# Seven block products from the third block on, earlier scores, and own banks for y: a retention layer and its feed-forward on one core

## The chip, the cores and the metric

The kernel runs on one NeuronCore of a Trainium2 chip. The core has five engines with queues of their own: TensorE (PE in the profile) multiplies matrices, its weight loads are listed apart (PEld); VectorE (DVE), ScalarE (ACT) and GpSimd (POOL) work element by element; SyncE (SP) issues transfers, which 16 DMA engines carry out. Each engine takes its own instructions in order and waits on semaphores for the others. The metric is the time of one execution in device microseconds; three runs before the change took 208.76, 208.87 and 209.04 us, median 208.87.

## The reference

Four sequences of 768 steps with eight heads of 64 go through a recurrent state that decays by a factor of its head; the result, with the heads side by side, is the input of a two-layer feed-forward net with g = h·tanh(softplus(h)) (Mish).

```python
gamma = 1.0 - 2.0 ** (-5.0 - np.arange(H))
for t in range(S):
    state = gamma[None, :, None, None] * state + np.einsum('bhd,bhe->bhde', k[:, :, t], v[:, :, t])
    y[:, :, t] = scale * np.einsum('bhd,bhde->bhe', q[:, :, t], state)
...
x = np.ascontiguousarray(attn_out.transpose(0, 2, 1, 3)).reshape(B * S, H * D)
h = x @ w_in
sp = np.where(h > 20.0, h, np.log1p(np.exp(np.minimum(h, 20.0))))
g = h * np.tanh(sp)
return (g @ w_out).astype(np.float32)
```

q, k and v are 4 x 8 x 768 x 64, w_in is 512 x 2048, w_out 2048 x 512, the output 3072 x 512, all float32.

## The kernel before

**Chunks and blocks.** The 3072 steps are 24 chunks of 128, six to a sequence. Chunks are grouped into blocks: block 0 has four (0 to 3), blocks 1 to 10 have two each: block 1 has 4 and 5, block 2 has 6 and 7, block 3 has 8 and 9, and so on to block 10 with 22 and 23. Blocks are numbered from 0 here, so the third block is block 2. The code's `first[blk]` is a block's first chunk, `a` or `g` a chunk.

**What a chunk needs first.** q, k and v are loaded (line 128, on SP's queue, three transfers of 256 KB), cast to 16 bits with their decay factors on GpSimd (`casts`, lines 223 to 231), and q and k are turned (transposed) by a DMA on SP's queue (`turn_by_dma`, line 235). This text calls the turn of chunk n by DMA Tn; there are 18, T6 to T23. `next_chunk(g)` casts up to chunk g, issues Tg and then loads further chunks, so many ahead of g as `load_to` says: chunks below g+3, g+4 or g+5. Stores of finished output tiles (line 179) go through the same SP queue. They are put on a list with a unit number and are issued by `store_due` when the program reaches that unit.

**A block's attention.** `get_ready(blk)` puts on TensorE the outer products k·v (u, line 401) and the scores k·q (at, line 394) of both chunks; the scores read the turned q and k. `settle` then works on DVE: `mid` and `sth` (lines 436, 438, 445, 447: the states in the middle and at the end of a chunk) and `am`, the masked scores (line 459). `leave` makes the state after the block's second chunk (nothing for the last chunk of a sequence). `retain` multiplies the states with q (`past_of`), `finish` the masked scores with v (`present_of`); both add up in y in PSUM, which is then copied to xt, the input of the feed-forward net: one half by DVE (line 526), one by ACT (line 528). `retain` also has a one-element copy to `seen` on DVE (line 514).

**A block's feed-forward.** The first product is cut in units: each unit (`g1`, line 541) is eight matmuls of 128x256 for two rows of h, followed by Mish on ACT (line 549). Blocks 1 to 10 have eight units, numbered 0 to 7. In blocks 1 and 2 the second product is 32 matmuls of 128x512 in eight more units, 8 to 15 (`g2_mm`, line 555; `g2_out`, line 559 copies the result out). From block `SEVEN` = 3 on it is made in the manner of Strassen and Winograd with seven products of half size, 56 matmuls of 128x256 (`seven`, line 615). It needs sums of g made on DVE: S1 and S2 in halves in `sums_a` (lines 604, 605), S3 in `sums_b` (609), S4 in `sums_c` (613), all in the tile gsum; sums T1 to T4 of the second weight (`weight_sums`, eight operations, lines 588 to 591, tile tmat), made once in the block before the first that uses them; and snapshots of partial results on ACT (line 641). Its order on TensorE is A11·B11, A12·B21, S1·T1, S2·T2, then the `retain` of the next block, S3·T3, the `finish` of the next block, S4·B22, A22·T4.

**Who comes when.** `manual_schedule` keeps the order of the program on each engine. `plan_of(blk)` says at which unit of a block the next block's attention, casts, turns and loads are put between the units. In block 1 that is get_ready at unit 10, in block 2 at unit 7, in blocks 3 to 6 at unit 3. From block `ONE` = 6 on the scores of the block after next are put into the seven products, interleaved with the states of the next (`retain` with `later`), and `settle` follows at unit 0 of the next block.

**PSUM.** The pool mm has three banks for h, o and the y of `seven`'s blocks; px has one bank; at has two tiles of two banks each, for the scores, u and the y of blocks 2 and 3. Tiles of a pool take its banks in turn, and a tile waits until the last reader of the bank's former tile is done.

Of the kernel before, what the change touches and what calls it, by code (L numbers as in the profile page):

```python
# [16 lines left out]
def kernel(  # L17
# [12 lines left out]
    P = 128  # L30
# [80 lines left out]
    loaded, cast, qkts, ats, ams, states, mids, us, ys = {}, {}, {}, {}, {}, {}, {}, {}, {}  # L111
    xts, gts, wins, wouts, wtmps = {}, {}, {}, {}, {}
    gtiles, tmats, gsums = {}, [], []
    SEVEN, ONE = 3, 6
    nload, ncast = [0], [0]
    stores = []

# [314 lines left out]
    def mid_of(g):  # L432
        u = us[g]
        mid = stp.tile([P, HP, D], FP16, name="mid")
        if g % NCH == 0:
            nc.vector.tensor_copy(mid, u[:, 0])  # L436
        else:
            nc.vector.tensor_tensor(mid, u[:, 0], states[g - 1], op=ALU.add)  # L438
        mids[g] = mid

    def state_of(g):
        u = us.pop(g)
        if not last_of_batch(g):
# [3 lines left out]
            nc.vector.tensor_tensor(st, su, gch, op=ALU.mult)  # L447
            states[g] = st

    def settle(blk):  # L450
        a = first[blk]
        at, u = held.pop(blk)
        for j in range(2):
            us[a + j] = u[:, :, j]
        mid_of(a)
        state_of(a)
        mid_of(a + 1)
        am = tpp.tile([P, 2, 2, HP, D], FP16, name="am")
        nc.vector.tensor_tensor(  # L459
            am.rearrange("p a j i c -> p (a j i) c"), at.rearrange("p a j i c -> p (a j i) c"),  # L460
            tri_half.unsqueeze(1).broadcast_to((P, 4 * HP, D)), op=ALU.mult)
        for j in range(2):
            ams[a + j] = am[:, :, j]

    def get_ready(blk):
        hold(blk)
        run(ready(blk, True), ready(blk, False))
        settle(blk)

    def leave(blk):  # L470
        state_of(first[blk] + 1)
# [29 lines left out]
    def retain(blk, later=None, spread=False):  # L501
        if spread:
            ys[blk] = [
                mmps.tile([P, 2, HP, D], FP32, name="y_ps", tag="mm") for _ in range(2)]
        else:
            y = pair_tile(atps, "y_ps", "at")
            ys[blk] = [y[:, s] for s in range(2)]
        if later is None:
            run(past_of(blk))
        else:  # L510
            hold(later)
            run(past_of(blk), ready(later, False))

        nc.vector.tensor_copy(seen, ys[blk][1][:, 1, 0, :1])
        if later is not None:
            run(ready(later, True))
            finish(blk, False)
# [40 lines left out]

    def g2_out(o_ps, blk, t, due, cols=slice(None)):
        osb = op.tile(list(o_ps.shape), FP32, name="osb", tag="osb")  # L560
        nc.vector.tensor_copy(osb, o_ps)
        if blk == 0:
            dst = out[:TB].rearrange("(p r) c -> r p c", r=CPB)[t]
        else:
            row0 = (first[blk] + t) * P
            dst = out[row0:row0 + P, cols]
        stores.append((due, dst, osb))
# [44 lines left out]
        (_, s2, _, s4), _, a12, _, _ = sum_views(blk)  # L612
        nc.vector.tensor_tensor(s4, a12, s2, op=ALU.subtract)

    def seven(blk, hooks, last):
        n, hf = NFB // 2, d_model // 2
        px = pxps.tile([P, hf], FP32, name="o_ps", tag="px")
        pb = mmps.tile([P, hf], FP32, name="o_ps", tag="mm")
        osb = [op.tile([P, d_model], FP32, name="osb", tag="osb") for _ in range(2)]

        def a(i, j):
            return lambda f: gts[blk, j * n + f][:, i * P:(i + 1) * P]

        def b(i, j):
            return lambda f: wouts[(i * n + f) // FPS][:, f % FPS, j * hf:(j + 1) * hf]

        def s(i):
            return lambda f: gsums[blk % 2][:, i - 1, f]

        def t(i):  # L630
            return lambda f: tmats[(i - 1) // 2][:, (i - 1) % 2, f]

        def mm(o_ps, x, w, first=False):
            for f in range(n):
                nc.tensor.matmul(  # L635
                    o_ps, x(f), w(f), start=first and f == 0, stop=f == n - 1,
                    skip_group_check=True)

        def snap(o_ps):
            x = op.tile([P, hf], FP32, name="snap", tag="snap", bufs=3)  # L640
            nc.scalar.copy(x, o_ps)  # L641
            return x

        def done(i, j, o_ps, plus=None):
            dst = osb[i][:, j * hf:(j + 1) * hf]
            if plus is None:
                nc.vector.tensor_copy(dst, o_ps)
            else:
                nc.vector.tensor_tensor(dst, o_ps, plus, op=ALU.add)  # L649
            row0 = (first[blk] + i) * P  # L650
            if last:
                nc.sync.dma_start(out[row0:row0 + P, j * hf:(j + 1) * hf], dst)

        mm(px, a(0, 0), b(0, 0), True)
        m1 = snap(px)
        mm(pb, a(0, 1), b(1, 0), True)
        sums_b(blk)
        done(0, 0, pb, m1)
        pe = mmps.tile([P, hf], FP32, name="o_ps", tag="mm")
        mm(pe, s(1), t(1), True)  # L660
        m5 = snap(pe)
        mm(px, s(2), t(2))
        u2 = snap(px)
        for fn, *args in hooks[0]:
            fn(*args)
        sums_c(blk)
        mm(px, s(3), t(3))
        done(1, 1, px, m5)
        for fn, *args in hooks[1]:
            fn(*args)  # L670
        mm(pe, s(4), b(1, 1))
        done(0, 1, pe, u2)
        mm(px, a(1, 1), t(4))
        done(1, 0, px)
        if not last:
            for i in range(2):
                row0 = (first[blk] + i) * P
                stores.append((1 + i, out[row0:row0 + P], osb[i]))
# [102 lines left out]
    def next_chunk(g):  # L781
        if g < NCK:
            cast_to(g + 1)
            turn_by_dma(g)
            if g < first[ONE] + 5:
                load_to(g + 3 if g < first[ONE] + 2 else g + 4)
            else:
                cast_to(g + 2)
                load_to(g + 5)

    def plan_of(blk):
        a = first[blk] + 4
        if blk >= SEVEN:
            plan = {u: [] for u in (0, 1, 3, 4, 7)}
            if blk > ONE:
                if blk + 1 < len(BLOCKS):
                    plan[0] = [(settle, blk + 1), (leave, blk + 1)]
            else:
                plan[3] = [(get_ready, blk + 1), (leave, blk + 1)]
            if blk >= ONE:  # L800
                plan[1] = [(next_chunk, a + 1)]
            else:
                ua, ub = (0, 4) if blk == ONE - 1 else (1, 7)
                plan[ua] += [(cast_to, a + 1), (next_chunk, a)]
                plan[ub] += [(cast_to, a + 2), (next_chunk, a + 1)]
            return plan
        early, then_seven = blk == 1, blk + 1 == SEVEN
        plan = {1: [(cast_to, a + 1)],
                (1 if early else 2 if then_seven else 4): [(cast_to, a + 1), (next_chunk, a)],
                (5 if early else 8): [(cast_to, a + 2), (next_chunk, a + 1)]}  # L810
        plan[10 if early else 7] = [(get_ready, blk + 1)]
        plan[13 if early else 12] = [(retain, blk + 1)]
        plan[14 if early else 13] = [(finish, blk + 1), (leave, blk + 1)]
        return plan

    first_block()
    for blk in range(1, len(BLOCKS)):
        n1 = NFB * BLOCKS[blk] // CPB
        last = blk + 1 == len(BLOCKS)
        plan = plan_of(blk)  # L820
        extra = weight_sums(0) + weight_sums(1) if blk + 1 == SEVEN else []
        for u in range(n1 if blk >= SEVEN else 2 * n1):
            store_due(u)
            if u < n1:
                g1(blk, u)
                if blk >= SEVEN and u in (5, 7):
                    sums_a(blk, (u - 5) // 2)
            else:
                t, part = divmod(u - n1, 4)
                if part == 0:  # L830
                    o_ps = mmps.tile([P, d_model], FP32, name="o_ps", tag="mm")
                for fb in range(part * 4, part * 4 + 4):
                    g2_mm(o_ps, blk, t, fb)
                if part == 3:
                    g2_out(o_ps, blk, t, u + 3 if t == 0 else 3)
            for fn, *args in plan.get(u, ()):
                fn(*args)
            if extra:
                extra.pop(0)()
        if blk >= SEVEN:  # L840
            hooks = [[], []]
            if not last:
                later = blk + 2 if ONE <= blk < len(BLOCKS) - 2 else None
                hooks = [[(retain, blk + 1, later, True)] + (
                            [(next_chunk, first[blk] + 6)] if blk >= ONE - 1 else []),
                         [(finish, blk + 1)] if later is None else []]
            seven(blk, hooks, last)
    store_due(2 * NFB)


# [28 lines left out]
```

## Time and profile before

| what | before |
|---|---|
| median of 3 runs | 208.87 us (208.76 to 209.04) |
| the profiled execution's own time | 208.58 us |
| its span, first to last instruction | 206.5 us |
| PE busy | 198.6 us, 96% of the span, 2605 matmuls |
| PEld busy | 147.5 us, 71% |
| DVE busy | 118.7 us, 57% |
| ACT busy | 84.6 us, 41% |
| POOL busy | 79.2 us, 38% |
| granted TensorE clock | 1.000 |
| SP's DMA queue | 96704 packets, 37.50 MB |

The profiled execution is one of many; its time exceeds its span by what lies before the first and after the last instruction. Busy shares are averages over the span. The chain of waits, followed back from the last instruction, is 75% TensorE, 9% DVE, 6% transfers and 6% SP's queue.

Two more views give the durations used later. DVE's rows are 0.42 us for a mid, 0.41 to 0.43 for suh, 0.42 to 1.13 for sth, 1.21 for am, 0.42 to 1.26 for a half sum (128x512), 0.68 to 0.91 for S3 and S4. GpSimd takes 1.04 us for a cast of q or v and 1.5 for one of k. The transfers of a turn took 3.1 to 6.9 us from issue to landing, 4.6 in the median.

### The profile page before, as it was taken

Reading aid. Unit: us, or ns where it says so; the run is one execution under the profiler, and the core shown is the slowest. Engines: PE = TensorE matmul, PEld = TensorE weight load, DVE = VectorE, ACT = ScalarE, POOL = GpSimd, SP = SyncE. Lnnn points to the kernel's source line nnn. Section 1 sums busy time; section 2 is a strip of 40 time slices with the busy share of each in tenths; the row PEclk is TensorE's granted clock in tenths of the full one; section 3 lists DMA queues with packets and bytes.
Section 4 is the critical chain, followed back from the end, with each engine's and each line's share of the span. In section 5 each row is a group of like instructions: output and inputs, shape, how many; then the busy total and the mean of one; then the engine's idle time right before and its main releaser. Section 6 shows DMA issues by size and latency. Waiting matters only on the chain.

```text
span 206.5 us, 5987 instructions
## 1 busy us (share of the span) xinstructions
PE 198.6 (96%) x2605; PEld 147.5 (71%) x2605; DVE 118.7 (57%) x211; ACT 84.6 (41%) x149; POOL 79.2 (38%) x82
## 2 busy tenths in 40 slices
PE   7999999999998899999999999999999999999993
PEld 2555444454864674788888887888888888888873
DVE  2697454267107999476388298296863853555152
ACT  2244665043530450352453452453363453542630
POOL 3246000426867266774466595098920000000000
PEclk9999999999999999999999999999999999999999
DMA  5999999999899999999999999999990500201102
GB/s 177 236 216 344 380 387 355 231 296 204 177 209 281 187 199 207 212 186 255 244 197 215 167 219 237 173 186 230 215 196 3 152 3 3 102 3 54 51 25 76
DMA packets 99993, 38.68 MB, mean 187 GB/s; under 512 B 90496, under 2 KB 94080, under 8 KB 99968
## 3 DMA queue, kind: packets, MB, share of 16 engines
q1 hardware_dynamic: 96704, 37.50, 89.0%
q10 hardware_dynamic: 3264, 0.81, 2.3%
q8 instruction: 20, 0.33, 0.7%
q14 instruction: 5, 0.04, 0.1%
HBM read 27.29 MB, written 6.29 MB: 163 GB/s over the span
## 4 chain that ended last, share of the span: by engine, by line
PE 75%; DVE 9%; DMA 6%; SPq 6%; ACT 1%; issue 1%; DVEq 0%; ACTq 0%
PE h_ps L541 37%; PE o_ps L635 22%; PE o_ps L555 8%; SPq L128 5%; PE y_ps L475 4%; DMA wi<-in_moe_w_in_dram 3%; DMA kf<-in_k_dram 3%; DVE gsum L604 2%; DVE am L459 2%; PE u_ps L401 2%; DVE sth L447 1%; DVE mid L438 1%; PE at L394 1%; DVE suh L445 1%; DVE gsum L605 1%
## 5 line engine op out<-in xcount | busy, mean ns | idle before, releaser
L541 PE MATMUL h_ps<-xt,win 128*128 128x256 f16 (+1 forms) x704 | 86.3, 282 | 1.1 <-ACT xt L528 0.5
L541 PEld LDWEIGHTS <-win 128*128 128x128 f16 x704 | 68.4, 98 | 17.3 <-issue 1.7
L549 ACT ACTIVATE g<-h_ps 128x512 f16<-128x512 f32 x96 | 57.3, 597 | 47.6 <-PE h_ps L541 47.6
L223 POOL TENSOR_TENSOR qk<-qf,qvs 128x512 f16<-128x512 f32 x20 | 22.1, 1107 | 50.0 <-DMA qf<-in_q_dram 34.0
L229 POOL TENSOR_TENSOR v<-vf,qvs 128x512 f16<-128x512 f32 x24 | 25.5, 1064 | 17.1 <-DMA vf<-in_v_dram 15.6
L555 PE MATMUL o_ps<-wout,g 128*128 128x512 f16 x128 | 30.0, 380 | 0.0
L228 POOL TENSOR_SCALAR qk<-kf 128x512 f16<-128x512 f32 x18 | 28.0, 1555 | 3.5 <-DMA kf<-in_k_dram 2.1
L635 PEld LDWEIGHTS <-gsum 128*128 128x128 f16 x256 | 23.9, 98 | 4.7 <-DVE gsum L604 1.1
L635 PE MATMUL o_ps<-tmat,gsum 128*128 128x256 f16 x192 | 24.0, 273 | 0.7 <-ACT snap L641 0.5
L555 PEld LDWEIGHTS <-g 128*128 128x128 f16 x128 | 11.7, 98 | 12.6
L635 PEld LDWEIGHTS <-g 128*128 128x128 f16 x192 | 18.8, 98 | 2.2
L604 DVE TENSOR_TENSOR gsum<-g 128x512 f16<-128x512 f16 x16 | 9.7, 603 | 14.2 <-ACT g L549 14.2
L528 ACT CAST xt<-y_ps 128x512 f16<-128x512 f32 x12 | 6.7, 588 | 25.7 <-DVE xt L526 16.0
L641 ACT COPY snap<-o_ps 128x256 f32<-128x256 f32 x24 | 8.9, 373 | 18.0 <-PE o_ps L635 18.0
L649 DVE TENSOR_TENSOR osb<-o_ps,snap 128x256 f32<-128x256 f32 x24 | 10.1, 422 | 9.1 <-ACT xt L528 3.1
L635 PE MATMUL o_ps<-wout,g 128*128 128x256 f16 x128 | 15.3, 273 | 0.0
L438 DVE TENSOR_TENSOR mid<-u_ps,sth 128x256 f16<-128x256 f32 x15 | 6.4, 423 | 10.7 <-PE u_ps L401 10.4
L249 PE MATMUL at<-ident 128*128 128x512 f16 (+1 forms) x34 | 10.8, 448 | 1.4 <-POOL ident L84 1.4
L459 DVE TENSOR_TENSOR am<-at,tri_half 128x1024 f16<-128x1024 f32 x9 | 10.9, 1214 | 0.0
L447 DVE TENSOR_TENSOR sth<-suh,gch 128x256 f16<-128x256 f32 x15 | 9.7, 649 | 0.6
L226 ACT ACTIVATE qk<-kf 128x512 f16<-128x512 f32 x6 | 3.8, 631 | 12.4 <-DMA kf<-in_k_dram 12.4
L436 DVE CAST mid<-u_ps 128x256 f16<-128x256 f32 x3 | 1.3, 422 | 12.9 <-PE u_ps L401 12.9
(79 smaller groups left out, 175.0 us busy)
## 6 DMA issues: line engine op xcount, KB each, us to landing
kf<-in_k_dram SPq DMA_DIRECT2D x23, 256.0 KB, 5.5
vf<-in_v_dram SPq DMA_DIRECT2D x23, 256.0 KB, 5.3
out_dram<-osb SPq DMA_DIRECT2D x22, 256.0 KB, 4.6
qf<-in_q_dram SPq DMA_DIRECT2D x19, 256.0 KB, 5.1
wt<-in_moe_w_out_dram SPq DMA_DIRECT2D x3, 1024.0 KB, 10.1
wi<-in_moe_w_in_dram SPq DMA_DIRECT2D x4, 512.0 KB, 7.2
wi<-in_moe_w_in_dram SPq DMA_DIRECT2D x2, 1024.0 KB, 10.8
qfirst<-in_q_dram SPq DMA_DIRECT2D x2, 512.0 KB, 4.9
```

Of the source, the lines that this page charges most:

```text
L128: queue.dma_start(loaded[g][n], (q, k, v)[n][b, :, c * C:(c + 1) * C].rearrange("h p d -> p h d"))
L223: nc.gpsimd.tensor_tensor(q16, qf, qs.unsqueeze(2).broadcast_to((P, H, D)), op=ALU.mult)
L228: nc.gpsimd.tensor_scalar(k16, kf, BOOST, None, op0=ALU.mult)
L229: nc.gpsimd.tensor_tensor(v16, vf, vs.unsqueeze(2).broadcast_to((P, H, D)), op=ALU.mult)
L249: nc.tensor.matmul(ats[g][:, 0, :m], ident, ident.unsqueeze(1).broadcast_to((P, m, P)), start=True, stop=True)
L447: nc.vector.tensor_tensor(st, su, gch, op=ALU.mult)
L459: nc.vector.tensor_tensor(am.rearrange("p a j i c -> p (a j i) c"), at.rearrange("p a j i c -> p (a j i) c"), tri_half.unsqueeze(1).broadc ...
L541: nc.tensor.matmul(h_ps[:, j], wins[s][f // 2][:, bp, f % 2 * P:(f % 2 + 1) * P], xts[blk][:, bp, :nt], start=(bp == 0), stop=(bp == NBP - 1))
L549: nc.scalar.activation(gt, h_ps, AF.Mish, scale=inv_boost3)
L555: nc.tensor.matmul(o_ps, gts[blk, fb][:, t * P:(t + 1) * P], wouts[s][:, f, cols], start=(fb == 0), stop=(fb == NFB - 1))
L604: nc.vector.tensor_tensor(s1, a21, a22, op=ALU.add)
L635: nc.tensor.matmul(o_ps, x(f), w(f), start=first and f == 0, stop=f == n - 1, skip_group_check=True)
```

## The change

Seven products are used from block 2 on, and `ONE` moves from 6 to 5. Blocks 2 and 3 become `tight`: the next block's get_ready stands at unit 5 of the first product, the masks (split off from `settle` as `mask_two`) go into `seven` behind the second product's sums, the halves of S1 and S2 follow units 6 and 7, and `leave` follows `finish`. In blocks 4 and 5 get_ready, masks and leave stand at unit 1. `load_to`'s distance follows `ONE`: five ahead from chunk 17 on instead of 19, four at chunk 16 alone. The y of a block made ready in block 1 gets a bank of mm and the bank of px, one for each half, instead of a two-bank tile of at. In `seven` the copy of the first result stands ahead of S3, and in the last block S2·T2 goes ahead of S1·T1. The first output tile of block 1 is copied by ACT. The weight sums, made in the block ahead of the first with seven products, move with it to block 1.

```diff
-    SEVEN, ONE = 3, 6
+    SEVEN, ONE = 2, 5
...
+    def get_ready(blk):
+        hold(blk)
+        run(ready(blk, True), ready(blk, False))
+        settle(blk)
+
     def settle(blk):
         a = first[blk]
-        at, u = held.pop(blk)
+        u = held[blk][1]
         for j in range(2):
             us[a + j] = u[:, :, j]
         mid_of(a)
         state_of(a)
         mid_of(a + 1)
+
+    def mask_two(blk):
+        at = held.pop(blk)[0]
         am = tpp.tile([P, 2, 2, HP, D], FP16, name="am")
         nc.vector.tensor_tensor(
...
-    def get_ready(blk):
-        hold(blk)
-        run(ready(blk, True), ready(blk, False))
-        settle(blk)
...
         else:
-            y = pair_tile(atps, "y_ps", "at")
-            ys[blk] = [y[:, s] for s in range(2)]
+            ys[blk] = [
+                pool.tile([P, 2, HP, D], FP32, name="y_ps", tag=tag)
+                for pool, tag in ((mmps, "mm"), (pxps, "px"))]
...
-        nc.vector.tensor_copy(osb, o_ps)
+        if blk > 0 and t == 0:
+            nc.scalar.copy(osb, o_ps)
+        else:
+            nc.vector.tensor_copy(osb, o_ps)
...
-    def seven(blk, hooks, last):
+    def seven(blk, masks, hooks, last):
...
         mm(pb, a(0, 1), b(1, 0), True)
+        done(0, 0, pb, m1)
         sums_b(blk)
-        done(0, 0, pb, m1)
+        for fn, *args in masks:
+            fn(*args)
         pe = mmps.tile([P, hf], FP32, name="o_ps", tag="mm")
+        if last:
+            mm(px, s(2), t(2))
+            u2 = snap(px)
         mm(pe, s(1), t(1), True)
         m5 = snap(pe)
-        mm(px, s(2), t(2))
-        u2 = snap(px)
+        if not last:
+            mm(px, s(2), t(2))
+            u2 = snap(px)
...
-            if g < first[ONE] + 5:
-                load_to(g + 3 if g < first[ONE] + 2 else g + 4)
-            else:
+            if g >= first[ONE] + 5:
                 cast_to(g + 2)
-                load_to(g + 5)
+            load_to(g + (3 if g < first[ONE] + 4 else 4 if g < first[ONE] + 5 else 5))
+
+    def tight(blk):
+
+        return SEVEN <= blk < SEVEN + 2
...
+        if blk < SEVEN:
+            return {1: [(next_chunk, a)],
+                    5: [(next_chunk, a + 1)],
+                    10: [(get_ready, blk + 1), (mask_two, blk + 1)],
+                    13: [(retain, blk + 1)],
+                    14: [(finish, blk + 1), (leave, blk + 1)]}
+        plan = {u: [] for u in (0, 1, 4, 5, 7)}
+        if tight(blk):
+            plan[5] = [(get_ready, blk + 1)]
+        elif blk <= ONE:
+            plan[1] = [(get_ready, blk + 1), (mask_two, blk + 1), (leave, blk + 1)]
+        elif blk + 1 < len(BLOCKS):
+            plan[0] = [(settle, blk + 1), (mask_two, blk + 1), (leave, blk + 1)]
+        if blk >= ONE:
+            plan[1] += [(next_chunk, a + 1)]
+        else:
+            ua, ub = (0, 4) if blk == ONE - 1 else (1, 7)
+            plan[ua] += [(next_chunk, a)]
+            plan[ub] += [(next_chunk, a + 1)]
         return plan
...
-                if blk >= SEVEN and u in (5, 7):
-                    sums_a(blk, (u - 5) // 2)
+                if blk >= SEVEN and u in ((6, 7) if tight(blk) else (5, 7)):
+                    sums_a(blk, u // 7)
...
-            seven(blk, hooks, last)
+            if tight(blk):
+                hooks[1].append((leave, blk + 1))
+            seven(blk, [(mask_two, blk + 1)] if tight(blk) else [], hooks, last)
```

The chunks' casts keep their order on GpSimd. In SP's queue the order is the same up to T13 and the loads behind it. There T14 and its loads go ahead of a store; T17 goes ahead of a store; the loads of chunk 21 go ahead of T18 and those of chunk 22 ahead of T19. From T20 on the order is the same again.

More of the change, by code (lines that the diff above doesn't have):

```diff
@@ L462, in settle @@
         for j in range(2):
-            ams[a + j] = am[:, :, j]
-    def get_ready(blk):
-        hold(blk)
-        run(ready(blk, True), ready(blk, False))
-        settle(blk)
+            ams[first[blk] + j] = am[:, :, j]
     def leave(blk):
@@ L784, in next_chunk @@
             turn_by_dma(g)
-            if g < first[ONE] + 5:
-                load_to(g + 3 if g < first[ONE] + 2 else g + 4)
-            else:
+            if g >= first[ONE] + 5:
                 cast_to(g + 2)
-                load_to(g + 5)
+            load_to(g + (3 if g < first[ONE] + 4 else 4 if g < first[ONE] + 5 else 5))
+    def tight(blk):
+        return SEVEN <= blk < SEVEN + 2
     def plan_of(blk):
         a = first[blk] + 4
[L793 to L813, printed above, removed]
+        if blk < SEVEN:
[4 more added lines that the diff above has]
+                    14: [(finish, blk + 1), (leave, blk + 1)]}
```

## The prediction, made before the changed kernel ran

> **What bounds the kernel now.** I read the page's tenths of the span first, then the chain of waits for the length of each block, then the timelines of TensorE and of SP's queue, then the landings of single transfers. The tenths and the kinds of DMA:
>
> ```profile
> PE   7999999999998899999999999999999999999993
> DMA  5999999999899999999999999999990500201102
> ```
>
> TensorE is busy nearly always, and the 16 DMA engines are too, until three quarters of the span (155 us). So there are two bounds side by side: TensorE's work, and the rate at which loads, turns and stores pass. The chain gives the starts of the blocks (h_ps pieces; start, length):
>
> ```profile
> 51.61 7.15 PE h_ps L541 x64
> 68.79 7.15 PE h_ps L541 x64
> 84.82 3.49 PE h_ps L541 x32
> 99.87 3.49 PE h_ps L541 x32
> 114.84 3.49 PE h_ps L541 x32
> 130.58 3.49 PE h_ps L541 x32
> 146.19 6.99 PE h_ps L541 x64
> 200.12 0.38 ACT snap L641
> ```
>
> Blocks 1 to 6 last 17.18, 16.03, 15.05, 14.97, 15.74 and 15.61 us, block 7 lasts 14.52 (to 160.71). The last line is a wait for a snapshot in the last block: the chain resumes on TensorE at 200.55, after products that ended at 200.10, so 0.45. TensorE's own idle times in block 1:
>
> ```profile
> 65.39 0.31 PE L475 MATMUL y_ps<-qkt,mid 64*64 64x64 f16 x8 [0.68 <-DVE am L459]
> 68.79 7.15 PE L541 MATMUL h_ps<-xt,win 128*128 128x256 f16 x64 [0.52 <-ACT xt L528]
> ```
>
> And SP's queue with three transfers that decide below (start, issue time):
>
> ```profile
> 69.10 2.40 SPq L235 DMA_TRANSPOSE qkt<-qk  x1
> ...
> 134.85 1.34 SPq L235 DMA_TRANSPOSE qkt<-qk  x1
> ...
> 139.31 0.88 SPq L128 DMA_DIRECT2D vf<-in_v_dram  x1
> ```
>
> They are T9, T19 and the load of v of chunk 22. From issue to landing they took 6.9, 5.6 and 4.8 us, so they landed at 76.0, 140.4 and 144.1. T9's answer is the one to check:
>
> ```profile
> L235 SPq DMA_TRANSPOSE qkt<-qk x1: 2396/2396/2396, 69.1 to 69.1; - x1
> ...
> DMA to landing us min/median/max: 6.9/6.9/6.9
> ```
>
> TensorE began the scores that need T9 and T8 here, T9's in the second half:
>
> ```profile
> 76.14 0.46 PE L394 MATMUL at<-qkt 64*64 64x64 f16 x32
> ```
>
> So T9 is just in time today. SP issues one transfer behind another with gaps of about 0.1 from 78.6 to 150 (one of 0.88 at 98.67); five of them (a chunk's turn, three loads, a store) take about 6.2 us, from T12's landing to T17's and in between. I take this as the transfers' own rate: what stands later in SP's queue lands later by 1.2 us a place.
>
> **The change, part by part, on TensorE.** Block 1: y in its own banks no longer waits for am (0.68 gone; mid, which it still needs, ended at 64.20 and TensorE is there at 64.70), and DVE and ACT copy the two halves of xt side by side, as they do in block 3 (both at 98.10), instead of one after the other (0.52 gone): −1.2. The eight weight sums (lines 588 to 591) move from block 2 to block 1, 52.4 on, where DVE idled 9.44 us. Their eight rows of today add to 8.4 us (0.68 to 1.53 each, the long ones beside GpSimd's casts), which ends at 60.8, before DVE's next work at 61.81; at 1.53 each it would be 64.6 and am late by up to 2, which the wait for T9 below would swallow. GpSimd's queue keeps its order; the casts of chunk 7 would be up to 1 us longer beside the sums, as 70.81 (1.53 for 1.04) and 72.42 (1.81 for 1.5) show, and T7 landed 1.4 before its scores (60.2 for 61.6). ACT's copy of osb (a 128x512 copy is 0.59 in xt's row) lies in its 8.76 us idle: nothing.
>
> Block 2: 56 matmuls of 128x256 at 0.109 (3.49 / 32) for 32 of 128x512 at 0.221 (4.42 / 20): 6.1 for 7.1. Put otherwise, it becomes a block like block 3, 15.05 for 16.03: −0.98. What it adds on DVE: half sums, sums and snapshots as block 3 has them; am moves behind the half sums (−1.2 ahead of them) while the scores move two units later (+1.75), so the half sums come 0.5 later against TensorE than in block 3 today, where they ended 0.9 before they were needed. I take 0.1 for block 2 and 0.3 for block 3 (0 to 1 each: in block 6 today the four took 3.7 us for 1.8 and TensorE waited). The state of chunk 9 (suh 0.41, sth 0.43 to 1.13) now stands between xt and the copy that frees the bank of block 3's first unit; that copy ended 0.35 before the need in block 3 today: 0.5 (0.1 to 1.2).
>
> Blocks 5 and 6: scores at unit 1 give DVE 1.75 more than unit 3 did, so block 5's wait on the sums (about 0.8) goes, and block 6 becomes one like block 7: −0.8 and −1.1. The last block takes S2·T2 before S1·T1, so the snapshot hides behind eight matmuls: −0.45; S2 was ready at 198.14 and TensorE is there at 198.34.
>
> The sum without transfers: −1.2 − 0.98 + 0.6 + 0.3 − 0.8 − 1.1 − 0.45 = −3.6.
>
> **The change on SP's queue.** Scores of block 3 are asked for at unit 5 of block 2 instead of unit 7. Block 2 would start at 67.6, its six units end at 72.84 (48 x 0.109), and T9's scores are due at 73.3. But nothing ahead of T9 in SP's queue moves: the same transfers in the same order, and none of them waits for anything of block 2. T9 lands at 76.0 still, and TensorE, which takes its queue in order, stands 2.7 us; units 6 and 7, ACT's g and the sums behind them stand too. From there: 76.25, + 1.83 (two units) + 3.49 + 0.62 + 0.98 + 0.38 + 1.87 (block 3's pieces) + 0.6 gives 86.0 for block 3's start (84.82 today), then 101.35, 116.3, 131.25 for blocks 4, 5 and 6. T11, T13 and T15 landed at 87.4, 99.0 and 111.5, some us ahead of their new dues (91, 103 and 118).
>
> T17 and T19 are another matter. With ONE one block earlier, load_to runs five ahead from chunk 17 on, not 19, so the three loads of chunk 21 pass T18 and those of chunk 22 pass T19. T17 goes one place earlier (lands 126.4 to 128.6; due in block 5's products at 127.9, so 0 to 0.7). T19 goes three places later: to the place that v of chunk 22 has today, after the very same set of transfers, so it lands not at 140.4 but at about 144.1, or 143.2 if the 0.88 gap before T14 (a store that now stands behind it) comes back. I take 143.7. TensorE needs it at 131.25 + 6.99 + 3.49 + 0.4 = 142.1, amid y of block 7, so it waits 1.6, and behind it stand the rest of y of block 7, the product S3·T3 and, on DVE, seen and S4. After T19's scores there are 3.8 us to block 7 (142.4 to 146.19 today), so block 7 starts at 147.5, +1.3; then nothing but the last block's −0.45.
>
> **Sum:** 206.5 + 1.3 − 0.45 = 207.35 of span against 206.5, +0.85. The profiled execution took 208.58 (2.1 outside its span); the runs' median is 208.87, so I add to that: 209.7. Since TensorE waits at T19, what blocks 1 to 5 gain or lose changes nothing until they lose 1.6 more; the number is T19's landing + 66.0.
>
> **The rivals.**
> (A) No transfer gates: the queue has slack that its issue times hide, and T9 and T19 come 3 us early. For it: latency fell to 3.7 at T15. Against it: DMA's row of nines. −3.6 to −4: 205.
> (B) T9 gates, T19 doesn't, landing by 142.1 (queue 2 us faster than now after the T9 stall, since stores no longer hold it): 86.0 and onward as above, −0.85 at the end: 208.0. This is faster, and it decides as soon as T19 lands before 142.4.
> (C) DVE is late: GpSimd's casts stretch the sums in blocks 2 to 5 by 0.8 each as in block 6 today; 3.2 less the 1.6 hidden: 211.3.
> (D) A stall slows the clock. The rows show 1.00 in every stretch and no wait of TensorE above 0.68, so they cannot say; if 3.4 us after T19's wait ran at half speed, +1.7: 211.4. The Trainium skill ("TensorE: Matmul & The Clock Gate", Part 1: The HAM clock gate) says that an idle window of some 3.4 us halves the clock until a busy one has passed. By that rule 2.7 and 1.6 us are just too short, and no run here shows it.
>
> **How the numbers follow.** Forecast 0.58 (its own range 209.0 to 210.6, from T19 between 143.0 and 144.6), A 0.08, B 0.14, C 0.12, D 0.08. About 0.2% (0.42 us) is what a measurement tells from no change here: below 208.45 is faster, above 209.29 slower. Faster: A and most of B, 0.2. Same: the rest of B and T19 before 143.2, 0.18. Slower 0.62. The range 208.0 to 211.3 leaves out A, some of B, and the tops of C and D.
>
> **What would show it.** In the changed profile: a wait of TensorE of 2 to 3 us at the first scores on qkt in block 2 around 73 to 76; T19 issued near 139 and landing near 144; a wait of 1 to 2.5 us amid y_ps in block 6; no am wait at block 1's y; no snapshot wait at 200. Wrong if T19 lands before 142, if block 3 starts before 85, or if a wait on sums over 1 us shows in blocks 2 to 5.

## The result: 207.81 us, faster by 0.4%, and the profile after

The changed kernel took 207.81 us in the median of 20 runs (205.87 to 210.04), the kernel before 208.78 in 20 runs: 0.97 us faster in the medians, a ratio of 0.9957 [0.9936, 0.9978], which leaves out the one slow run (210.04). The forecast was 0.8 slower. The profiled execution took 207.79 us with a span of 206.0; the one before had 208.58 and 206.5.

TensorE's waits by releaser (line, total us, times, longest us):

```profile
PE at L394 <- DMA qkt<-qk: 3.4, 2, 1.9
PE at L249 <- POOL ident L84: 1.3, 1, 1.3
```

The first row is new: twice the scores wait for a turn, 3.4 us together. The waits of block 1 on am and on xt's second half, and that of the last block on a snapshot, which the kernel before showed, are not in the view. Both places in TensorE's timeline (start, length, the wait ahead in brackets):

```profile
75.14 0.32 PE L394 MATMUL at<-qkt 64*64 64x64 f16 x16 [1.85 <-DMA qkt<-qk]
...
142.56 0.22 PE L394 MATMUL at<-qkt 64*64 64x64 f16 x2 [1.54 <-DMA qkt<-qk]
```

The first is T9 in block 2, the second T19 in block 6. They are also the two dents in the page's row of tenths for TensorE; DMA's row stays at nines:

```profile
PE   7998999999999969999999999997999999999993
DMA  5999999999899999999999999999980500200202
```

The chain of waits gives the blocks (start, length):

```profile
51.60 7.15 PE h_ps L545 x64
...
84.64 5.24 PE h_ps L545 x48
...
130.01 7.00 PE h_ps L545 x64
146.33 6.99 PE h_ps L545 x64
...
196.74 6.13 PE o_ps L642 x56
```

The last line is the last block's seven products in one piece of 56 matmuls: the snapshot's wait is gone. Before, block 3 began at 84.82, block 6 at 130.58, block 7 at 146.19. So the changed kernel reaches block 6 0.57 ahead and block 7 0.14 behind. What the new waits left of the gain is the last block's.

SP's queue around T19, and T19's own answer:

```profile
132.55 1.38 SPq L235 DMA_TRANSPOSE qkt<-qk  x1
...
138.22 1.30 SPq L235 DMA_TRANSPOSE qkt<-qk  x1
```

```profile
  PE at L394: 1.5, 1
...
DMA to landing us min/median/max: 4.3/4.3/4.3
```

T18 and T19 are issued some 5 and 3.4 us later than before (127.70 and 134.85). T19 lands at 142.5, and who waited for it is TensorE at the scores.

### The profile page after: what moved, and what is told of

Read it like the earlier page. It is cut to its first block, busy times and chain, and to the rows that moved or that the text cites. A ratio compares the mean times of both kernels' runs of the same rounds, so it can differ in the third digit from the quotient of the medians.

```text
span 206.0 us, 6051 instructions
## 1 busy us (share of the span) xinstructions
PE 196.5 (95%) x2629; PEld 149.9 (73%) x2629; DVE 120.9 (59%) x217; ACT 86.7 (42%) x154; POOL 79.0 (38%) x82
## 4 chain that ended last, share of the span: by engine, by line
PE 77%; DMA 12%; SPq 7%; ACT 1%; DVE 1%; issue 1%; ACTq 0%
PE h_ps L545 38%; PE o_ps L642 26%; PE o_ps L559 6%; SPq L128 6%; DMA qkt<-qk 5%; PE y_ps L478 4%; DMA kf<-in_k_dram 3%; DMA wi<-in_moe_w_in_dram 3%; PE at L394 1%; PE u_ps L401 1%; SPq L146 1%; ACT xt L379 0%; SPq L187 0%; DVE win L163 0%; PE at L271 0%
## 5 line engine op out<-in xcount | busy, mean ns | idle before, releaser
L223 POOL TENSOR_TENSOR qk<-qf,qvs 128x512 f16<-128x512 f32 x20 | 22.7, 1135 | 50.1 <-DMA qf<-in_q_dram 37.6
L642 PEld LDWEIGHTS <-gsum 128*128 128x128 f16 x288 | 27.2, 98 | 3.5
L642 PE MATMUL o_ps<-tmat,gsum 128*128 128x256 f16 x216 | 26.4, 273 | 0.0
L642 PEld LDWEIGHTS <-g 128*128 128x128 f16 x216 | 21.1, 98 | 2.5
L559 PE MATMUL o_ps<-wout,g 128*128 128x512 f16 x96 | 22.6, 380 | 0.0
L648 ACT COPY snap<-o_ps 128x256 f32<-128x256 f32 x27 | 10.0, 372 | 19.4 <-PE o_ps L642 19.4
L656 DVE TENSOR_TENSOR osb<-o_ps,snap 128x256 f32<-128x256 f32 x27 | 11.4, 423 | 10.5 <-PE o_ps L642 4.8
L642 PE MATMUL o_ps<-wout,g 128*128 128x256 f16 x144 | 17.2, 273 | 0.0
L559 PEld LDWEIGHTS <-g 128*128 128x128 f16 x96 | 8.8, 98 | 9.4
L394 PE MATMUL at<-qkt 64*64 64x64 f16 x288 | 6.4, 195 | 3.4 <-DMA qkt<-qk 3.4
L642 PE MATMUL o_ps<-wout,gsum 128*128 128x256 f16 x72 | 9.4, 273 | 0.0
```

Of the source, the lines that this page charges most:

```text
L223: nc.gpsimd.tensor_tensor(q16, qf, qs.unsqueeze(2).broadcast_to((P, H, D)), op=ALU.mult)
L559: nc.tensor.matmul(o_ps, gts[blk, fb][:, t * P:(t + 1) * P], wouts[s][:, f, cols], start=(fb == 0), stop=(fb == NFB - 1))
L642: nc.tensor.matmul(o_ps, x(f), w(f), start=first and f == 0, stop=f == n - 1, skip_group_check=True)
```

## The experiments

The theory that stood after this result: T19's place in SP's queue sets the end, T9's wait is swallowed by T19's, and the gains of blocks 1 to 5 are real but hidden behind both. Rivals: the gain is less than summed because DVE or GpSimd takes it back; a wait slows TensorE's clock; the queue has nothing to do with it. The table has the readings on which the sections below rest. "To the end" is the span less block 7's start, all in us.

| kernel | wait at T9 / T17 / T19 | T19 lands | block 7 starts | to the end | span | median (ratio) |
|---|---|---|---|---|---|---|
| before | 0 / 0 / 0 | 140.4 | 146.03 | 60.5 | 206.5 | |
| changed | 1.85 / 0 / 1.54 | 142.5 | 146.17 | 59.8 | 206.0 | 207.81 (0.9957) |
| loads_as_before | 1.40 / 0 / 0 | 138.0 | 144.27 | 59.8 | 204.1 | 206.21 (0.9893) |
| before_far_loads | 0 / 0 / 0.39 | 143.0 | 146.63 | 60.5 | 207.1 | 209.04 (1.0021) |
| stores_later | 0 / 1.96 / 0 | 143.2 | 147.04 | 59.9 | 206.9 | 208.65 (0.9979) |
| stores_later_loads_three | 0 / 0 / 0 | 136.6 | 143.31 | 59.9 | 203.2 | 204.47 (0.9799) |

Block 7's starts in this table are from TensorE's timeline; the chain puts the same starts up to 0.16 later.

### Only the loads put back: loads_as_before

The changed kernel with the distances of the loads as they were, so that T18 and T19 stand ahead of the loads of chunks 21 and 22 again.

```diff
-            load_to(g + (3 if g < first[ONE] + 4 else 4 if g < first[ONE] + 5 else 5))
+            load_to(g + (3 if g < 16 else 4 if g < 19 else 5))
```

> The changed kernel with the load distance of the kernel before (three ahead below chunk 16, four for 16 to 18, five from 19 on); the loads of chunks 21 and 22 then stand behind T18 and T19 again. Theory (T19's place in SP's queue sets the end): T19 lands some 3 us earlier, at 138.5 to 140, TensorE is there at 140.8, the wait of 1.54 us in block 6 is gone, block 7 starts at 144.8 instead of 146.3, and the time is about 206.3 us (ratio to before 0.988). Rival (the transfers as a whole are too slow, whatever their order): another turn, T18 or T20, is late instead, and the time stays at 207.8 us (ratio 0.995).

206.21 us in 9 runs, a ratio of 0.9893 [0.9859, 0.9928], 1.6 us faster than the changed kernel; the wait at T19 was 1.54. In the profile T19 landed at 138.0, and of the two waits one is left (TensorE's waits):

```profile
PE at L394 <- DMA qkt<-qk: 1.4, 1, 1.4
```

One line of loads decides over 1.6 us: what was forecast of T19 is right as a mechanism.

### Only the loads moved, in the kernel before: before_far_loads

```diff
-            if g < first[ONE] + 5:
-                load_to(g + 3 if g < first[ONE] + 2 else g + 4)
-            else:
+            if g >= first[ONE] + 5:
                 cast_to(g + 2)
-                load_to(g + 5)
+            load_to(g + (3 if g < 16 else 4 if g < 17 else 5))
```

> The kernel before with the load distance of the changed one alone (five ahead from chunk 17 on). Theory (T19's place): T19 lands at 142.5 to 144 instead of 140.4, TensorE needs it at 142.4, so it waits 0.1 to 1.6 us and the time is 208.9 to 210.4 us (ratio 1.001 to 1.008). Rival (the order of loads and turns is indifferent): no wait on a turn in block 6, ratio 1.000.

209.04 us in 12 runs, 1.0021 [0.9993, 1.0049]: the times can't tell the two expectations apart, the profile can. T19 was issued at 139.31 and landed at 143.0, 2.6 later than before; TensorE (timeline) came only 0.39 sooner:

```profile
143.02 0.22 PE L394 MATMUL at<-qkt 64*64 64x64 f16 x2 [0.39 <-DMA qkt<-qk]
```

The same order of loads costs 0.4 here and 1.5 in the changed kernel, because there TensorE is earlier. In both a late transfer costs what TensorE is ahead of it.

### The queue ahead of T9 lightened: stores_later and stores_later_loads_three

Block 0's stores are due at unit 6 of block 1 instead of unit 1, so four of them stand behind T9 instead of ahead of it (issued from 71.75 on; in the changed kernel from 60.48); eight buffers osb hold their tiles so long. In stores_later_loads_three the loads run three chunks ahead throughout, too.

```diff
-        osb = op.tile(list(o_ps.shape), FP32, name="osb", tag="osb")
+        osb = op.tile(list(o_ps.shape), FP32, name="osb", tag="osb", bufs=8)
...
-                    g2_out(o_tiles[t], 0, t, 1)
+                    g2_out(o_tiles[t], 0, t, 6)
```

and in the second also

```diff
-            load_to(g + (3 if g < first[ONE] + 4 else 4 if g < first[ONE] + 5 else 5))
+            load_to(g + 3)
```

> The changed kernel with the four stores of block 0 put at unit 6 of block 1 instead of unit 1, so that they stand behind T8 and T9 (eight tiles for osb instead of five). Theory (T9 gates block 2, but T17 and T19 gate behind it): T9 lands about 2.5 us earlier, the wait of 1.85 us in block 2 is gone and block 3 starts at about 82.8 instead of 84.6; but T17 and T19 keep their places, so waits of 1.5 to 2 us in block 5 and of some us at T19 in block 6 take it back, block 7 starts at 146.3 as now, and the time stays at 207.8 us (ratio to before 0.995). Rival (TensorE's sum sets the end, each wait counts by itself): 206.0 us (ratio 0.987).

208.65 us in 12 runs, 0.9979 [0.9950, 1.0008]: the 0.995 expected stands at the interval's lower end, the rival's 0.987 below it. T9 landed at 71.3 and nothing waited for it; block 3 began at 83.23, 1.24 ahead of the changed kernel. The lead lasted until block 5. There T17 landed at 127.1, and TensorE had to wait (timeline):

```profile
127.15 0.22 PE L394 MATMUL at<-qkt 64*64 64x64 f16 x2 [1.96 <-DMA qkt<-qk]
...
128.12 1.75 PE L642 MATMUL o_ps<-tmat,gsum 128*128 128x256 f16 x8
129.66 1.92 PE L642 MATMUL o_ps<-wout,gsum 128*128 128x256 f16 x8
```

Eight matmuls of 128x256 take 1.04 elsewhere; here they took 1.75 and 1.92. The windows around it show why (stretch, length, then busy time of PE, PEld, DVE, ACT and POOL, and after these the granted clock, DMA's share and GB/s):

```profile
127.00:128.00 1.00, 0.85 (x73) 0.85 (x74) 0.51 (x2) 0.00 (x0) 0.92 (x2) 1.00 1.25 217
128.00:129.00 1.00, 1.00 (x26) 0.75 (x13) 0.86 (x1) 0.72 (x2) 0.31 (x1) 0.66 1.34 226
129.00:130.00 1.00, 1.00 (x7) 0.73 (x5) 0.04 (x1) 0.35 (x1) 0.03 (x1) 0.50 1.01 164
130.00:131.00 1.00, 1.00 (x7) 0.69 (x6) 0.39 (x1) 0.00 (x0) 1.00 (x1) 0.50 0.83 189
131.00:132.00 1.00, 1.00 (x8) 0.76 (x7) 0.32 (x1) 0.00 (x0) 0.92 (x2) 0.64 0.83 187
```

The granted clock fell to a half: 0.68 us of the second stretch, all of the third and fourth and 0.72 of the fifth, 3.4 us in all, which costs 1.7 of work. Block 5 lasted 19.17; the changed kernel's 15.36 plus 1.96 plus 1.7 is 19.0. So a wait removed upstream came back as a longer one downstream, with a slower clock behind it. The wait at T19 that was expected too did not come: T19 landed at 143.2, and TensorE was late itself.

> The changed kernel with the stores of block 0 behind T9 and with loads three chunks ahead throughout, so that T9, T17, T18 and T19 all move to earlier places. Theory (turns gate, by their places in SP's queue): no wait on a turn above 0.3 us anywhere; the waits of 1.85 and 1.54 us go and block 5 loses none, so block 7 starts at about 142.9 and the time is 204.4 us (ratio to before 0.979). Rival (another bound is close behind, sums on VectorE or loads that now come late for the casts): 205.5 to 207 us, with waits on sums or casts in their place.

204.47 us in 5 runs, 0.9799 [0.9769, 0.9829]: 2% faster than the kernel before and 3.3 us below the changed one. T17 landed at 123.2, T18 at 130.0, T19 at 136.6, and TensorE's longest waits are those of the start:

```profile
PE at L249 <- POOL ident L84: 1.4, 1, 1.4
PE h_ps L545 <- DVE win L163: 0.9, 1, 0.9
```

With every turn on time the change is worth 4.4 us in the medians. Neither half did it alone: the stores alone left T17 late (a wait of 1.96), the loads put back left T9 late (1.40). The later stores with the old load distances, three to five chunks, were not run.

### Single parts in the kernel before: own banks, the queue, the last block

before_own_banks gives only the y of block 2 (made in block 1) its own banks:

```diff
+        elif blk == 2:
+            ys[blk] = [
+                pool.tile([P, 2, HP, D], FP32, name="y_ps", tag=tag)
+                for pool, tag in ((mmps, "mm"), (pxps, "px"))]
```

> The kernel before with own banks for the y of block 2 alone (one bank of mm, one of px). Theory (the two waits of block 1 go, but T9 stands close behind): waits of 0.68 and 0.52 us in block 1 are gone, block 2 starts 1.2 us earlier, at about 67.6; its scores on T9 are then due at 75.0 and T9 lands at 74.9 to 76.0, so 0 to 1 us comes back as a wait there; time 207.7 to 208.7 us, ratio to before 0.994 to 0.999. Rival (nothing is behind it): ratio 0.994 and no wait on a turn.

208.21 us in 11 runs, 0.9958 [0.9939, 0.9976]. The two expectations overlap there, so the ratio alone settles nothing; the profile does. No turn was waited for, as the rival had it. Block 1 lasted 15.85, for 17.18 in the first profile of the kernel before (the changed kernel's block 1, 15.77, has the gain too). But that 17.18 was unusually long: in four other profiles of kernels whose block 1 waits for am as before (before_again, before_far_loads, before_last_swap, before_queue_relief) it lasted 16.66 to 16.79, and the wait on am, 0.68 in the first, was 0.15 to 0.26. before_again has

```profile
65.34 0.31 PE L475 MATMUL y_ps<-qkt,mid 64*64 64x64 f16 x8 [0.16 <-DVE am L459]
```

In the first profile the state ahead of am (sth, at 62.80) took 0.95 us, in before_again 0.42. So own banks are worth 0.8 to 0.9 in block 1, not 1.3, and the medians differ by as much (208.98 to 208.21). Block 5 lasted 16.41 for 15.74 in the first profile. On TensorE:

```profile
124.49 1.48 PE L639 MATMUL o_ps<-tmat,gsum 128*128 128x256 f16 x12 [0.43 <-DVE gsum L608]
...
126.75 0.31 PE L475 MATMUL y_ps<-qkt,mid 64*64 64x64 f16 x8 [0.54 <-DVE osb L653]
```

Both waits are for DVE, whose sums in this block look so:

```profile
122.09 1.26 DVE L608 TENSOR_TENSOR gsum<-g 128x512 f16<-128x512 f16 x1
123.38 0.71 DVE L609 TENSOR_TENSOR gsum<-gsum,g 128x512 f16<-128x512 f16 x1
124.02 0.41 DVE L608 TENSOR_TENSOR gsum<-g 128x512 f16<-128x512 f16 x1
124.47 0.42 DVE L609 TENSOR_TENSOR gsum<-gsum,g 128x512 f16<-128x512 f16 x1
124.81 1.56 DVE L613 TENSOR_TENSOR gsum<-g 128x1024 f16<-128x1024 f16 x1
```

The undisturbed rows of the same shapes are 0.42 and 0.68. GpSimd's casts of one chunk ran at 121.84 (q, 1.23), 123.15 (k, 1.55) and 124.78 (v, 1.04); each of the three long sums began shortly after one of them, while the two short ones ran in the later part of k's. This is not the edit's doing as far as the runs show: before_again, where nothing is edited, has 16.42 in block 5.

before_queue_relief is the kernel before with both edits of stores_later_loads_three:

```diff
...
-                    g2_out(o_tiles[t], 0, t, 1)
+                    g2_out(o_tiles[t], 0, t, 6)
...
-                load_to(g + 3 if g < first[ONE] + 2 else g + 4)
...
-                load_to(g + 5)
+            load_to(g + 3)
```

> The kernel before with the stores of block 0 behind T9 and the loads three chunks ahead throughout, as in the fastest kernel so far. Theory (the kernel before waits for no turn, so earlier turns are worth nothing to it; the 4.4 us come from TensorE's work and waits that the change removes): T9, T17 and T19 land 3 to 5 us earlier, ratio 1.000, time 208.8 us. Rival (the relief of the queue is itself the gain): about 205 us, ratio 0.98.

208.01 us in 12 runs, 0.9958 [0.9935, 0.9981]: neither 1.000 nor 0.98. T9, T17 and T19 landed 5 to 7 us earlier, and no turn was waited for in either profile, so the queue's relief gave TensorE nothing through the turns, as the theory has it. Against the first profile block 1 is 0.39 shorter (16.79, as in the repeats) and block 5 0.5 (15.24 for 15.74). In block 5 the half sums were not drawn out by casts:

```profile
122.66 0.41 DVE L604 TENSOR_TENSOR gsum<-g 128x512 f16<-128x512 f16 x1
123.11 0.42 DVE L605 TENSOR_TENSOR gsum<-gsum,g 128x512 f16<-128x512 f16 x1
```

The cast of q began at 123.92 here, as the load that it waits for landed later, not at 122.77; it drew out S3 instead (1.53 at 124.25). In five other profiles of the kernel before or with one part changed (the first, again, own banks, last swap, far loads) block 5 lasted 15.74, 16.42, 16.41, 15.89 and 16.18. That the time at which the casts come is the reason is likely, but nothing was run that moves only it.

before_last_swap puts S2·T2 ahead of S1·T1 in the last block:

```diff
+        if last:
+            mm(px, s(2), t(2))
+            u2 = snap(px)
         mm(pe, s(1), t(1), True)
         m5 = snap(pe)
-        mm(px, s(2), t(2))
-        u2 = snap(px)
+        if not last:
+            mm(px, s(2), t(2))
+            u2 = snap(px)
```

> The kernel before with S2·T2 ahead of S1·T1 in the last block alone. Theory: the wait of 0.45 us on the snapshot goes, nothing takes its place, last copy on VectorE 0.45 us earlier; ratio 0.998, time 208.4 us. Rival (S2's second half or the first snapshot is late instead): ratio 1.000 with a wait on one of them in the last block.

208.39 us in 12 runs, 0.9971 [0.9954, 0.9988], and the products run through without a wait (timeline):

```profile
198.40 2.78 PE L635 MATMUL o_ps<-tmat,gsum 128*128 128x256 f16 x24
```

From block 7's start to the end this profile has 59.85 for 60.47, as all kernels with the swap do (the table): 0.62 gained where the profile had shown a wait of 0.46. This part, at the end with nothing behind it, is kept in full (0.59 in the medians).

### The same kernels again: how far a landing scatters

Three more profiles of the changed kernel and one of the kernel before, nothing edited.

> The changed kernel once more, unaltered, for the scatter of the two landings. Theory (T19's landing sets the end): the span is T19's landing + 63.5 (142.5 + 63.5 = 206.0 in the first profile), within 0.4, wherever between 141 and 144.5 it lands; T9's landing (75 to 76) moves block 3's start and nothing behind T19. Rival (DVE or an earlier block sets the end): the span follows block 3's start, and the rest from T19's landing to the end moves by 1 us or more between profiles.

> The same a second time. Theory: span = T19's landing + 63.5 within 0.4. If T19 lands near 143.7, as forecast, the span is 207.2, and the forecast's error was the landing of one execution; if it lands at 142 to 142.8 in all three, the forecast's place in the queue was priced too high. A mean granted clock below 0.995 would show its slow stretch behind T9's wait (75 to 79 us), where the later wait swallows it.

> The same a third time; span = T19's landing + 63.5 within 0.4 by the theory, and by the rival a remainder that moves by 1 us or more.

> The kernel before once more, for the place in the queue from which the forecast took T19's landing: v of chunk 22, the third load behind T19, which landed at 144.1 in the profile shown. If its landing is a property of the order, 143.8 to 144.4 again; if it depends on the execution, it is off by 1 us or more, while the span stays 206.0 to 207.0, since nothing waits for it there.

The changed kernel took 208.29, 207.70 and 207.56 us, with spans of 206.5, 205.9 and 205.8. T19 landed at 143.0, 142.4 and 141.2. In the first and second, landing + 63.5 is 206.5 and 205.9, as the theory says. In the second the first product of block 1 began 1.0 later than in the first profile (52.62 for 51.60), and this cost nothing: TensorE's timeline has less of a wait at T19 instead.

```profile
142.45 0.22 PE L394 MATMUL at<-qkt 64*64 64x64 f16 x2 [0.55 <-DMA qkt<-qk]
```

The third breaks the rule: 141.2 + 63.5 is 204.7, and the span was 205.8. There T19 gated nothing, because TensorE was late itself. Its wait at T9 was 1.87, about as long as in the first profile (1.85), but behind it the clock fell (windows; columns as above):

```profile
75.00:76.00 1.00, 1.00 (x24) 0.88 (x25) 0.97 (x3) 0.00 (x0) 0.00 (x0) 1.00 1.35 217
76.00:77.00 1.00, 1.00 (x9) 0.80 (x7) 0.44 (x2) 0.60 (x1) 0.68 (x1) 0.70 1.35 218
77.00:78.00 1.00, 1.00 (x7) 0.69 (x5) 0.00 (x0) 0.28 (x1) 0.92 (x2) 0.50 1.25 249
78.00:79.00 1.00, 1.00 (x7) 0.67 (x6) 0.62 (x2) 0.31 (x1) 0.95 (x1) 0.50 1.16 317
79.00:80.00 1.00, 1.00 (x7) 0.72 (x6) 0.23 (x1) 0.37 (x1) 0.97 (x1) 0.59 1.37 211
```

Block 3 began at 85.94 for 84.46 in the first of the three, and TensorE reached T19's scores at 142.31 without a wait. From these scores to the end all four profiles have the same 63.45 (within 0.05): 142.56, 143.05, 142.45 and 142.31 to 206.0, 206.5, 205.9 and 205.8. So the theory holds in a wider form: the end is 63.45 behind the later of two, T19's landing and TensorE's arrival, and in these four profiles TensorE came from 2.04 ahead of the landing to 1.1 behind it.

The kernel before took 209.28 us, with a span of 207.3, outside the 206.0 to 207.0 expected. In the place from which T19's landing was taken, v of chunk 22 landed at 145.1 for 144.1. Its TensorE waited 1.03 for a half sum in block 5, and no turn was waited for:

```profile
125.98 1.49 PE L635 MATMUL o_ps<-tmat,gsum 128*128 128x256 f16 x12 [1.03 <-DVE gsum L604]
```

## Why the prediction was wrong

Its main mechanism, a late T19 that swallows the gains ahead of it, was right; the size of T19's landing was off, and on that size hung the sign.

- **The step that failed: "it lands not at 140.4 but at about 144.1, or 143.2 if the 0.88 gap before T14 comes back. I take 143.7."** T19 landed at 142.5, 143.0, 142.4 and 141.2 in four profiles. The gap did come back: before, SP stood still for 0.88 ahead of a store; now T14 stands ahead of it and the queue goes on without a gap, and T15 was issued at 106.67 for 107.79. So the lower of the two figures was the right branch, and splitting the difference was not called for. Another 0.5 is the transfer itself: a turn from 138.22 took 4.3 us, where 4.8 of a load of v had been taken. For the last 0.2 the queue was ahead before that (T13 issued at 94.47 for 94.73). And the figure came from one execution, without its scatter: 1 us between two profiles of the kernel before.
- **"It waits 1.6" came out as 1.54,** but for another reason than a sum that held: TensorE was at the scores at 141.0, not 142.1, so both sides of the subtraction were 1.1 to 1.2 too late.
- **From T19's landing to the end: 63.65 forecast, 63.45 measured.** With that remainder the span equals the former 206.5 if T19 lands at 143.05. The forecast stood 0.65 behind this point, the measurement 0.55 ahead of it: an error of 1.2 us in a time near 143 turned the sign.
- **T9: lands at 76.0, wait 2.7, block 3 at 86.0.** It landed at 75.1, and the wait was 1.85; block 3 began at 84.64 by the chain, which is the prediction's own sign against it (before 85). The queue ahead was indeed unchanged; four profiles of the changed kernel gave 74.9 to 75.8. That none of it would matter at the end held in three of four profiles.
- **The costs on DVE, 0.6 and 0.3, were not there.** The largest part, 0.5, was for a copy that frees the bank of block 3's first unit and now stands behind the state of chunk 9. It does stand there (DVE's timeline):

```profile
83.48 0.41 DVE L445 TENSOR_TENSOR suh<-u_ps,mid 128x256 f32<-128x256 f32 x1
83.93 0.56 DVE L447 TENSOR_TENSOR sth<-suh,gch 128x256 f16<-128x256 f32 x1
84.41 0.41 DVE L656 TENSOR_TENSOR osb<-o_ps,snap 128x256 f32<-128x256 f32 x1
```

  The copy ended at 84.82, but TensorE's timeline has block 3's first matmul at 84.47, without a wait. So, whatever frees that bank, the first unit does not wait for this copy, and the 0.5 was not paid (in stores_later_loads_three the same: the copy ended at 83.36, the matmul began at 83.15). Block 3 lasted 15.05, as before the change; 15.35 was forecast. The weight sums in block 1 ran from 52.27 to 60.86, ahead of mid at 61.80, as forecast.
- **The other gains.** Block 1: −1.2 forecast, 15.77 for 17.18 in the two profiles compared, but −0.9 against the 16.66 to 16.79 of four others: the wait on am was priced from one long one. Block 2 without its wait: 0.8 shorter in stores_later_loads_three (15.09 for 15.87), −0.98 forecast. Block 5: −0.8 forecast, −0.4 (15.36 for 15.74). Block 6 without a wait (loads_as_before): 14.61 for 15.61, −1.1 forecast. The last block: −0.45 forecast, 0.46 of wait gone and 0.62 of time; this is most of the 0.2 between 63.65 and 63.45. "The sum without transfers" was −3.6 of span; with all turns on time it was −3.3 (203.2 for 206.5), in an execution whose block 1 began 0.67 later.
- **From span to time.** 2.1 outside the span and 0.29 from the profiled time to the median had been added; the changed kernel has 1.8 and 0.02. This is 0.6 of the 1.9 by which 209.7 was off; 1.35 is the span (207.35 for 206.0), nearly all of it T19's landing.
- **The rivals.** A, that no transfer gates, fell: two did. B had the nearest number (208.0) from T9's wait alone, but T19 gated in three of four profiles. C, DVE late by 0.8 in each block, did not show. D was put behind T19's wait and was not seen there; behind T9's wait in one repeat, and behind T17's in stores_later, it was, with the price that it named, 1.7. Its reading that the kernel before waits nowhere above 0.68 leaves out 1.35 at the very start (for ident), behind which the granted clock was 1.00.

## What to carry to other kernels

Where the end hangs on when one transfer lands, work out the landing at which the change breaks even and set it against the scatter of that landing over several profiles: here the break-even was 143.05, the landings of one kernel lay from 141.2 to 143.0, and the spans of its 20 timed runs from 204.1 to 208.2, seven of them at or above the 206.5 of the profile before. No sign could be had from one execution. A gain on the busiest engine is only kept if every transfer that it will now meet earlier is moved forward with it; the whole change was worth 4.4 us once the turns stood ahead of loads that nobody needed yet, and 1.0 without. A part with nothing behind it, as in the last block, keeps its gain. A wait that was read in one profile should be looked up in a second before it enters a sum: block 1's on am was 0.68 once and 0.15 to 0.26 four times.

## What was not expected of the hardware

**A wait of TensorE of 1.9 us can halve its clock for 3.4 us.** It did so behind 1.96 (stores_later) and 1.87 (the third repeat), and did not behind 1.85 (the first profile of the changed kernel), 1.95 and 2.04 (the first repeat). The halved stretch began 1.2 and 1.5 us after the wait's end and lasted 3.4 us both times. Timed runs speak for the same: the mean granted clock was 0.99 in 8 of 20 runs of the changed kernel, 2 of 9 of loads_as_before (208.0 and 208.3 us, the others 205.5 to 206.9), 6 of 12 of stores_later and 1 of 12 of before_far_loads; it was 1.000 in all 5 of stores_later_loads_three and at least 0.997 in all runs of the kernel before that the record lists it for, and neither profile has such a wait. Which wait dropped it in a timed run isn't shown. The Trainium skill ("TensorE: Matmul & The Clock Gate", Part 1: The HAM clock gate) says that the clock halves after an idle window of about 3.4 us, and that the window runs freely, so that its effect varies between runs. The length of the halved stretch and the variation agree with this; that a window need be idle as a whole does not, since the waits were 1.9. How much of it has to be idle stays open: no run here varied the wait alone.

**A DVE operation on two tiles in SBUF takes up to three times as long when it begins during a cast on GpSimd, and the kind of cast matters.** In before_own_banks a half sum that began 0.25 into a cast of q (1.23 long) took 1.26 for 0.42, and S3, begun 0.03 into a cast of v, 1.56 for 0.68: longer by 0.84 and 0.88, where 0.98 and 1.01 of the cast were left. Beside the cast of k (1.55 long) a half sum begun 0.23 into it took 0.71, and those begun 0.87 and 1.32 into it the undisturbed 0.41 and 0.42. The long sth of block 1 in the first profile is of the same kind: 0.95 for 0.42, begun 0.38 into a cast of q. am, which reads PSUM, took 1.21 or 1.22 in block 1 of each of the six profiles of the kernel before and its variants. So what the casts cost depends on when they come in each execution: block 5 of the kernel before lasted 15.74 in one profile and 16.42 in another.
